# Chunk attention followed by a two-layer MLP: the same 1459 steps in another written order, and wider filler matmuls

## The chip, the cores and the metric

The kernel runs on one core of one Trainium2 chip. A core has a matrix engine (PE, with its weight loads shown as PEld), a vector engine (DVE), a scalar engine (ACT), a general engine (POOL), and a sync engine (SP) that issues transfers. POOL issues transfers too: each of its load instructions keeps POOL busy while it runs. The metric is the device time of one execution in microseconds (us); the time before is the median of three runs.

## The reference: what is computed

`q`, `k` and `v` have 8 batches, 8 heads, 576 rows and 64 columns. Attention is done inside chunks of 64 rows only, and its output, written as 4608 tokens of 512 columns, goes through two dense layers with a leaky ReLU between them:

```
scores = (q_c @ k_c.T) / sqrt(64)            # per chunk of 64 rows
attn   = exp(scores - max); attn /= sum + 1e-9
x      = (attn @ v_c) as 4608 tokens x 512
h      = x @ w_in                            # 512 -> 2048
out    = max(0.01 * h, h) @ w_out            # 2048 -> 512
```

## The kernel before: tiles, stages and what sets the order

**Attention.** The 4608 tokens are 36 groups of 128 tokens, numbered u = 0 to 35. A group passes through a fixed chain of steps, and the texts below use these names:

- the loads of q and k by POOL (L96), which cast from 4 to 2 bytes on the way; v comes per batch into `VB` (L120), for the first four groups per group into `v_t` (L126);
- the transposes of q and k: for u below 10 on PE (L410 for q, L415 for k; PSUM tiles `qp` and `kp`), after that as DMA transposes that SP issues (L438 for q into `QT`, L441 for k into `KT`); a copy puts q into the padded tile `QZ` (on POOL, L454, for u of 10 and above);
- s(u), the scores on PE (tile `Sp`, L466 and L473); then on DVE and ACT the row maximum, the subtraction, the exponential, the row sum, its reciprocal, and n(u), the scaling (tile `en`, L527, on DVE or POOL);
- the transpose of `en` into `et`: on PE (L535) for u below 8 and for u = 8, 9, 18, 27, 29, 31, and as a DMA transpose by SP (L546) for the others; this one is called d(u);
- v(u), the product with v on PE (tile `xp`, L558 and L571), whose result ACT or DVE copies into `xT`.

**The MLP.** The tokens are also cut into twelve blocks: four of 128 tokens, then eight of 512. The weights come as four column blocks of `w_in`, each in two halves (L135, 256 KB a half), and four blocks of `w_out` (L141, 512 KB each). Blocks 0 to 3 do plain products (L187 for the first layer, L215 for the second). Blocks 4 and 5 do the first layer plainly; from there on each layer of a block is done with seven products of halves in place of eight (L328 and L377), with sums of halves formed on DVE or POOL (L237, L240).

**The order.** Nothing is scheduled at run time. The program builds a list of 1459 steps, each with an engine; a table `ON` names the engine for those steps that could run on several. A second table, `ORDER`, is a written list: one entry per step with the step's number, the amount of filler to issue ahead of it, and the PSUM banks that it takes. `run` (L633) walks through it and emits the steps. An engine executes its own instructions in that order, so an entry says what stands ahead of what in the queue of its engine, and nothing else: SP's list is the order of the DMA transposes and of the stores, POOL's list is the order of the loads and of POOL's own work.

**Fillers.** `idle` (L590) issues matmuls of a constant tile of ones into a PSUM bank that nobody reads. They stand only in the first 20 us, ahead of PE steps that wait for their input.

```
(66, (13, 0), 0)    # step 66: the transpose of q of group 0, behind 13 filler matmuls into bank 0
```

Of the kernel before, what the change touches and what calls it, by code (L numbers as in the profile page):

```python
# [16 lines left out]
def kernel(  # L17
# [9 lines left out]
    nc = tc.nc  # L27
# [123 lines left out]
    ones = XF[0][:, 0, 0, :128]  # L151
# [15 lines left out]
    def bank(shape, name, tag):  # L167
        return psp.tile(shape, FP32, name=name, tag=tag, bufs=1)
# [421 lines left out]
    def idle(n, tag):  # L590
        t = bank([128, 4, 128], "idle", tag)
        for i in range(n):
            nc.tensor.matmul(out=t[:, i % 4, :], lhsT=ones, rhs=ones, start=True, stop=True)
# [95 lines left out]
    def arrive_v(b, c0, c1, after=(), **kw):  # L689
# [9 lines left out]
        ('ze', 0): 'dve', ('n', 0): 'dve', ('d2', 0): 'act', ('a', 0): 'act', ('out', 0, 0): 'act', ('p', 1, 0): 'act', ('k', 1): 'dve', ('ze', 1): 'act',  # L699
        ('n', 1): 'dve', ('d2', 1): 'act', ('a', 1): 'act', ('p', 2, 0): 'act', ('p', 2, 1): 'act', ('k', 2): 'act', ('ze', 2): 'act', ('n', 2): 'dve', ('d2', 2): 'dve',  # L700
        ('a', 2): 'act', ('out', 2, 0): 'act', ('p', 3, 0): 'dve', ('p', 3, 1): 'dve', ('k', 3): 'act', ('ze', 3): 'act', ('n', 3): 'dve', ('d2', 3): 'dve',
        ('a', 3): 'act', ('out', 3, 0): 'act', ('p', 4, 0): 'dve', ('p', 4, 1): 'act', ('k', 4): 'act', ('ze', 4): 'act', ('n', 4): 'dve', ('d2', 4): 'dve',
# [535 lines left out]
    for j in range(len(BLOCKS)):  # L1238
        groups((START[j] + BLOCKS[j]) // G)
        w = BLOCKS[j] / 512  # L1240
# [26 lines left out]
        for h, n in enumerate(parts):  # L1267
            p0, w = place + h / per_h, 1 / per_h
# [47 lines left out]
```

## Time and profile before

| what | value |
|---|---|
| median of 3 runs | 283.37 us (283.05 to 284.16) |
| the profiled execution, whole | 282.36 us |
| its span, first to last instruction | 280.6 us |
| PE busy in the span | 266.1 us (95%), 3480 matmuls |
| of it fillers | 96 matmuls, 8.6 us |
| DVE, ACT, POOL busy | 217.8, 177.8, 171.9 us |
| loads issued by POOL | 18.09 MB written, queue q0 |
| transposes and stores issued by SP | queue q1, 46544 packets |

The span is 1.8 us shorter than the execution's own time, because the time also holds what lies around the first and last instruction. In a line of the timeline the first number is the start from the span's beginning and the second how long the instruction or the run of equal instructions took; a bracket gives the idle time of the engine ahead of it and what ended it. In a table of stretches each engine has its busy time and, in brackets, its number of instructions.

### The profile page before, as it was taken

What the parts mean: (1) busy time and instruction counts of PE and PEld (TensorE: products, weight loads), DVE (VectorE), ACT (ScalarE), POOL (GpSimd) and SP (SyncE); (2) the same over time, 40 slices, a digit from 0 to 9 for tenths busy, and PEclk for the clock granted to TensorE, in tenths of its full rate; (3) what the DMA queues carried; (4) which work ended last, traced back from release to release, by engine and by line L of the source; (5) the groups of instructions that cost most, each with busy time, mean ns of one, the idle gap of its engine ahead of it and who ended that gap; (6) DMA issues with size and microseconds to landing.
All of it is one profiled execution on the core that took longest, in us unless ns stands there. A gap on an engine that the chain in (4) does not pass through costs nothing.

```text
span 280.6 us, 8400 instructions
## 1 busy us (share of the span) xinstructions
PE 266.1 (95%) x3480; PEld 239.3 (85%) x3480; DVE 217.8 (78%) x368; ACT 177.8 (63%) x356; POOL 171.9 (61%) x209
## 2 busy tenths in 40 slices
PE   4969999999999899998799999999999999999994
PEld 4859677889999799997799999998899999887883
DVE  3764357785898778999679998999899987688951
ACT  4464574878743476796588745999887765353412
POOL 8989965978999256695888387880763220350000
PEclk9997999999999999999999999999999999999999
DMA  9999999999999999999999999999992410002064
GB/s 129 140 164 195 179 172 172 130 157 171 169 139 157 136 131 134 197 184 120 156 140 176 151 175 140 169 295 146 113 138 21 168 22 18 2 0 77 0 227 151
DMA packets 162021, 38.29 MB, mean 136 GB/s; under 512 B 153024, under 2 KB 157632, under 8 KB 161984
## 3 DMA queue, kind: packets, MB, share of 16 engines
q0 software_dynamic: 114400, 18.09, 97.1%
q1 hardware_dynamic: 46544, 19.41, 44.2%
q8 instruction: 27, 0.44, 0.7%
q10 hardware_dynamic: 1040, 0.26, 0.4%
q14 instruction: 10, 0.08, 0.1%
HBM read 36.70 MB, written 9.44 MB: 164 GB/s over the span
## 4 chain that ended last, share of the span: by engine, by line
PE 73%; POOL 10%; DMA 10%; DVE 3%; issue 1%; ACT 1%; POOLq 0%; DVEq 0%
PE oA L377 15%; PE hA L328 14%; PE hT L187 10%; PE oC L377 9%; PE hC L328 7%; PE oP L215 5%; PE hB L328 4%; DMA KT<-k_in 4%; DMA w_inT<-in_moe_w_in_dram 3%; PE oB L377 3%; DMA et<-en 3%; POOL q_in L96 3%; POOL k_in L96 3%; PE Sp L473 2%; PE xp L571 2%; POOL QZ L454 2%
## 5 line engine op out<-in xcount | busy, mean ns | idle before, releaser
L377 PEld LDWEIGHTS <-gT 128*128 128x128 f16 x640 | 61.2, 98 | 6.7
L187 PE MATMUL hT<-xT,w_inT 128*128 128x128 f16 x768 | 48.5, 221 | 2.0 <-DMA w_inT<-in_moe_w_in_dram 2.0
L454 POOL COPY QZ<-QT 64x512 f16<-64x512 f16 x52 | 35.0, 674 | 21.2 <-DMA QT<-q_in 19.3
L187 PEld LDWEIGHTS <-w_inT 128*128 128x128 f16 x768 | 44.8, 99 | 2.8 <-issue 2.3
L328 PEld LDWEIGHTS <-VF 128*128 128x128 f16 x512 | 39.9, 98 | 3.7 <-issue 0.8
L527 POOL TENSOR_TENSOR en<-ex,zi 128x512 f16<-128x512 f16 x20 | 21.4, 1071 | 27.7 <-DVE zi L519 11.5
L240 DVE TENSOR_TENSOR tmp<-hC,tmp 128x512 f32<-128x512 f32 x48 | 32.1, 680 | 7.1 <-PE hC L328 4.3
L483 DVE TENSOR_REDUCE mx<-Sp 128x8 f32<-128x512 f32 x36 | 24.8, 688 | 15.8 <-PE Sp L473 14.4
L199 ACT ACTIVATE gT<-hT 128x512 f16<-128x512 f32 x48 | 27.0, 597 | 13.3 <-PE hT L187 12.7
L96 POOL DMA_DIRECT2D k_in<-in_k_dram x39 | 33.4, 862 | 2.1 <-ACT gT L199 1.2
L96 POOL DMA_DIRECT2D q_in<-in_q_dram x39 | 33.5, 863 | 1.2 <-DMA q_in<-in_q_dram 0.8
L377 PE MATMUL oA<-WF,gT 128*128 128x256 f16 x256 | 32.4, 273 | 0.0
L328 PEld LDWEIGHTS <-w_inT 128*128 128x128 f16 x384 | 29.9, 98 | 2.6 <-issue 0.5
L130 ACT ACTIVATE tmp<-hA 128x512 f32<-128x512 f32 x43 | 24.8, 597 | 10.5 <-PE hA L328 10.4
L493 ACT ACTIVATE ex<-sh 128x512 f16<-128x512 f32 x36 | 22.8, 632 | 8.5 <-DVE sh L487 8.3
L505 DVE TENSOR_REDUCE z<-ex 128x8 f32<-128x512 f16 x36 | 24.4, 678 | 4.2 <-ACT ex L493 4.1
L328 PE MATMUL hA<-XF,VF 128*128 128x128 f16 (+1 forms) x256 | 26.8, 246 | 0.6 <-DVE hB L132 0.6
L377 PEld LDWEIGHTS <-S 128*128 128x128 f16 x256 | 24.4, 98 | 2.6
L130 ACT ACTIVATE xT<-xp 128x512 f16<-128x512 f32 (+1 forms) x34 | 17.9, 548 | 13.6 <-PE xp L558 6.8
L487 DVE TENSOR_TENSOR sh<-Sp,mx 128x512 f32<-128x512 f32 x36 | 24.7, 685 | 0.5
L130 ACT ACTIVATE tmp<-oA 128x512 f32<-128x512 f32 (+1 forms) x16 | 8.6, 542 | 19.1 <-PE oA L377 19.1
L120 POOL DMA_DIRECT2D VB<-in_v_dram x16 | 17.7, 1105 | 4.3 <-PE xp L571 2.9
(93 smaller groups left out, 524.8 us busy)
## 6 DMA issues: line engine op xcount, KB each, us to landing
out_dram<-osb SPq DMA_DIRECT2D x14, 512.0 KB, 6.0
VB<-in_v_dram POOLq DMA_DIRECT2D x14, 288.0 KB, 12.2
q_in<-in_q_dram POOLq DMA_DIRECT2D x31, 128.0 KB, 10.4
k_in<-in_k_dram POOLq DMA_DIRECT2D x31, 128.0 KB, 9.6
w_inT<-in_moe_w_in_dram POOLq DMA_DIRECT2D x8, 256.0 KB, 8.7
w_outT<-in_moe_w_out_dram POOLq DMA_DIRECT2D x4, 512.0 KB, 8.5
out_dram<-osb SPq DMA_DIRECT2D x6, 256.0 KB, 4.8
v_t<-in_v_dram POOLq DMA_DIRECT2D x4, 128.0 KB, 6.5
```

The source lines that it names most:

```text
L96: nc.gpsimd.dma_start(out=t[a - u * G:z - u * G], in_=src[b, :, r:r + z - a, :].rearrange("h p d -> p h d"))
L130: nc.scalar.activation(out=to, in_=of, func=AFT.Copy, bias=0.0, scale=1.0)
L187: nc.tensor.matmul(out=hT[:, i, :], lhsT=w_inT[:, t, fc * 128:(fc + 1) * 128], rhs=xT[:, t, r0 % RING:r0 % RING + tb], start=(i == 0 and t ...
L199: nc.scalar.activation(out=to, in_=of, func=AFT.Prelu, bias=0.0, scale=1.0, alpha=0.01)
L240: (nc.vector if e == "dve" else nc.gpsimd).tensor_tensor(out=to, in0=a, in1=b, op=ALU.add)
L328: nc.tensor.matmul(out=PA[key][:, c, :], lhsT=w[:, t, fc * 128:(fc + 1) * 128], rhs=x[:, t, :], start=(m in (1, 5) and c == 0 and t == 0), ...
L377: nc.tensor.matmul(out=to, lhsT=lhs[:, fc, p * 128:(p + 1) * 128], rhs=rhs[:, fc, :], start=(fresh and fc == 0), stop=(fc == HB - 1), skip ...
L454: nc.gpsimd.tensor_copy(out=QZ[u % NQZ][part, :, :, s, :], in_=QT[u][part].rearrange("p i (e t) -> p i e t", e=2))
L483: nc.vector.tensor_reduce(out=MX[u], in_=SP[u], axis=AXL.X, op=ALU.max)
L487: nc.vector.tensor_tensor(out=SH[u], in0=SP.pop(u), in1=MX.pop(u).unsqueeze(2).to_broadcast((128, 8, CH)), op=ALU.subtract)
L493: nc.scalar.activation(out=E[u], in_=SH.pop(u), func=AFT.Exp, bias=0.0, scale=SCL)
L505: nc.vector.tensor_reduce(out=Z[c[0]][:, u - c[0]], in_=E[u], axis=AXL.X, op=ALU.add)
```

## The change

The steps, their arithmetic and their sizes stay. Three things differ.

**The filler.** The tile of ones grows from 128 to 512 columns (one memset in place of one), and an amount n is issued as single matmuls of up to four units of 128 columns:

```diff
-    ones = XF[0][:, 0, 0, :128]
+    ones = XF[0][:, 0].rearrange("p t n -> p (t n)")
     nc.vector.memset(ones, 1.0)
...
     def idle(n, tag):
-        t = bank([128, 4, 128], "idle", tag)
-        for i in range(n):
-            nc.tensor.matmul(out=t[:, i % 4, :], lhsT=ones, rhs=ones, start=True, stop=True)
+        t = bank([128, 512], "idle", tag)
+        while n:
+            w = min(n, 4) * 128
+            nc.tensor.matmul(out=t[:, :w], lhsT=ones[:, :128], rhs=ones[:, :w], start=True, stop=True)
+            n -= w // 128
```

The amounts: before 13, 1, 6, 8, 4, 5, 25, 15 and 19 (96 units, 96 matmuls); after 17, 8, 20, 9, 23, 14, 22 and 13 (126 units, 35 matmuls).

**The engines.** 95 of the entries of `ON` differ: 36 steps go from DVE to ACT and 36 from ACT to DVE, 12 from POOL to DVE and 9 from DVE to POOL, one from ACT to POOL and one back. Those that the prediction names:

```diff
-        ('n', 5): 'pool'
+        ('n', 5): 'dve'
...
-        ('n', 14): 'dve'
+        ('n', 14): 'pool'
...
-        ('sf', 9, 3): 'dve'
+        ('sf', 9, 3): 'pool'
...
-        ('sf', 10, 3): 'pool'
+        ('sf', 10, 3): 'dve'
```

(`sf` is the sum of halves of a whole block's activations, 128 x 2048, that opens or closes a second-layer product.)

**The order.** `ORDER` is replaced as a whole; its first lines as an example:

```diff
     ORDER = [
-        (51, 0), (10, 0), (6, 0), (2, 0), (1, 0), (35, 0), (0, 0), (37, 0), (36, 0), (66, (13, 0), 0), (7, 0), (50, 0), (40, 0), (68, (1, 1), 1), (67, 0), (43, 0),
-        (3, 0), (69, 0), (45, 0), (70, (6, 2), 2), (11, 0), (71, 0), (12, 0), (98, (8, 3), 3), (72, 0), (5, 0), (99, 0), (9, 0), (73, 0), (96, (4, 4), 4), (126, 0, 5),
...
+        (1, 0), (3, 0), (50, 0), (6, 0), (10, 0), (35, 0), (2, 0), (37, 0), (36, 0), (0, 0), (43, 0), (66, (17, 0), 0), (68, 0, 1), (45, 0), (7, 0), (67, 0), (40, 0),
+        (69, 0), (15, 0), (70, (8, 2), 2), (8, 0), (98, 0, 3), (71, 0), (46, 0), (126, 0, 4), (12, 0), (72, 0), (51, 0), (11, 0), (73, 0), (99, 0), (48, 0),
...
```

Read with the step numbers resolved, the lists of the engines differ in these places. POOL's first entries (q3 is the load of q of group 3, w0b the second half of `w_in` block 0, P0 block 0 of `w_out`, v8 a chunk of batch 0's v; memsets left out):

| | order of POOL's first loads |
|---|---|
| before | v_t1, q2, identity, k1, q1, k2, v_t0, q3, k3, w0b, w1b, w0a, w1a, q4, v_t2, w2b, v8b, w2a, P0, k4, P1, v_t3, q5, k5 |
| after | k1, v_t0, q2, v_t1, identity, q1, k2, v_t2, w1a, k3, q3, w0b, w0a, w2a, w1b, q4, q5, k5, w2b, P0, v8b, k4, P1, v_t3 |

PE's list from the first MLP product (A/B is block A, column block B of the first layer):

| | order on PE |
|---|---|
| before | 0/0, v(1), 0/1, q4 transposed, `en` of group 2 transposed, 1/0, v(2), 1/1, s(3), 2/0, 2/1, then 0/2 |
| after | v(1), 0/0, k3 transposed, `en` of group 2 transposed, 1/0, v(2), q4 transposed, 0/1, s(3), 2/1, 2/0, 1/1, then 0/2 |

SP's list between 84 and 129 us of the profile before (tk17 is the DMA transpose of k of group 17, tq that of q, store4b the second store of block 4):

| | order on SP |
|---|---|
| before | tk15, tk16, d11, tq17, d12, d13, d14, tk17, tq18, tk18, tq19, d15, tq20, tk19, store4a, tk20, tq21, store4b, d16, tk21, tq22, d17, tk22, d19 |
| after | tk15, d11, tk16, d12, tq17, d13, tk17, tq18, d14, tk18, d15, tq19, tq20, tk19, store4a, tk20, tk21, tq21, d16, tq22, d17, tk22, store4b, d19 |

Ahead of that, tk11 goes from in front of the stores of blocks 2 and 3 to behind them. On PE between 60 and 140 us the products with v and the scores move by up to 2.9 us of PE work against the MLP products around them: v(10) 1.98 us earlier, v(11) 1.79 us later, v(14) 2.89 us later, v(15) 2.89 us earlier, s(21) 1.97 us earlier, s(22) 0.87 us earlier (sums of the PE work that passes from one side of the step to the other, in the durations of the profile before).

More of the change, by code (lines that the diff above doesn't have):

```diff
@@ L694 @@
     ON = {
[4 rows of a table removed]
[L699 to L702, printed above, removed]
[55 rows of a table removed]
[4 rows of a table added]
+        ('d2', 0): 'act', ('a', 0): 'act', ('out', 0, 0): 'act', ('p', 1, 0): 'act', ('k', 1): 'dve', ('ze', 1): 'act', ('n', 1): 'dve', ('d2', 1): 'act',
+        ('a', 1): 'act', ('p', 2, 0): 'act', ('p', 2, 1): 'dve', ('k', 2): 'act', ('ze', 2): 'act', ('n', 2): 'dve', ('d2', 2): 'dve', ('a', 2): 'act',
+        ('out', 2, 0): 'act', ('p', 3, 0): 'dve', ('p', 3, 1): 'act', ('k', 3): 'act', ('ze', 3): 'dve', ('n', 3): 'dve', ('d2', 3): 'dve', ('a', 3): 'dve',
+        ('out', 3, 0): 'act', ('p', 4, 0): 'act', ('p', 4, 1): 'act', ('k', 4): 'dve', ('ze', 4): 'dve', ('n', 4): 'dve', ('d2', 4): 'act', ('a', 4): 'act',
[56 rows of a table added]
     }
     ORDER = [
[102 rows of a table removed]
[102 rows of a table added]
     ]
```

319 rows, old and new, of tables (ON, ORDER) are left out of this document.

## The prediction

> **What bounds the kernel now.** I read the page first, then the busy time by stretch, then the places on PE's timeline where a bracket shows idle time, and last what those waits lead back to on SP and POOL.
>
> ```profile
> PE 266.1 (95%) x3480; PEld 239.3 (85%) x3480; DVE 217.8 (78%) x368; ACT 177.8 (63%) x356; POOL 171.9 (61%) x209
> ...
> DMA  9999999999999999999999999999992410002064
> ```
>
> PE is the bound, and the transfer engines are busy in every slice up to about 210 us. Written order can't change PE's useful work, so the question is where PE is not busy:
>
> ```profile
> core 0: us, PE busy (x) PEld busy (x) DVE busy (x) ACT busy (x) POOL busy (x), PEclk, DMA share, GB/s
> 0.00:18.00 18.00, 13.28 (x192) 11.37 (x192) 10.86 (x25) 9.37 (x18) 16.81 (x27) 1.00 1.41 139
> 18.00:25.00 7.00, 5.44 (x91) 5.13 (x92) 2.23 (x6) 1.44 (x6) 5.78 (x9) 0.76 1.59 189
> 25.00:92.00 67.00, 67.00 (x1002) 58.12 (x1001) 48.41 (x81) 44.28 (x91) 57.74 (x71) 1.00 1.93 162
> 92.00:100.00 8.00, 6.72 (x108) 6.06 (x105) 5.89 (x12) 3.69 (x8) 2.79 (x5) 1.00 1.69 141
> 100.00:125.00 25.00, 25.00 (x406) 24.14 (x404) 22.23 (x41) 18.76 (x38) 17.04 (x22) 1.00 1.77 162
> 125.00:140.00 15.00, 12.66 (x193) 11.51 (x191) 11.83 (x20) 9.78 (x21) 10.78 (x12) 1.00 1.71 139
> 140.00:250.00 110.00, 110.00 (x1272) 100.27 (x1270) 95.91 (x159) 80.44 (x161) 59.78 (x69) 1.00 1.29 120
> 250.00:255.00 5.00, 4.06 (x36) 3.34 (x35) 4.96 (x7) 2.84 (x6) 1.18 (x1) 1.00 0.28 102
> ```
>
> There are four places. The start: loads have not come, and the clock was 0.76 between 18 and 25 us. Then 8.00 - 6.72 = 1.28 us between 92 and 100, 15.00 - 12.66 = 2.34 us between 125 and 140, and 5.00 - 4.06 = 0.94 us between 250 and 255. Everywhere else up to 255 us PE is full and nothing can be gained, only lost. So the change is worth at most 1.28 + 2.34 + 0.94 = 4.56 us behind the start, plus what the start gives.
>
> The change has three parts that can reach these places: the front (loads and fillers), the transfers and PE steps between 60 and 140 us, and the block sums near the end.
>
> **The front.** The fillers go from 96 units in 96 matmuls to 126 units in 35.
>
> ```profile
> 11.71 1.57 PE L593 MATMUL idle<-XF 128*128 128x128 f16 x25
> ...
> 19.15 1.05 PE L187 MATMUL hT<-xT,w_inT 128*128 128x128 f16 x16 [1.63 <-DMA w_inT<-in_moe_w_in_dram]
> ...
> 22.53 0.63 PE L410 MATMUL qp<-ident,q_in 128*128 128x128 f16 x4
> ...
> 25.98 3.74 PE L187 MATMUL hT<-xT,w_inT 128*128 128x128 f16 x64
> 29.56 1.03 PE L215 MATMUL oP<-w_outT,gT 128*128 128x512 f16 x4
> ```
>
> A filler unit costs 1.57 / 25 = 0.063 us, so 30 more cost 1.9 us of PE. They stand ahead of steps that wait anyway: the first MLP block began at 19.15 only because `w_in` had not landed, behind 1.63 us of idle PE. That wait covers them; without it the 1.9 us would be on the path. I take 0, with 0 to 0.4 should one batch outlast its wait.
>
> What decides is the order of POOL's loads. At the entry "0/2" of PE's list both versions have done the same useful steps, so its start compares the two fronts. Before, 64 matmuls take 29.56 - 25.98 = 3.58 us, a block of 16 takes 0.895, and 0/2, the third of them, starts at 25.98 + 2 x 0.895 = 27.77. After, PE reaches the transposition of q4 behind 0/0 and 1/0, and q4's load now has two more loads ahead of it, a `v_t` (128 KB) and a half block of `w_in` (256 KB):
>
> ```profile
> w_inT<-in_moe_w_in_dram POOLq DMA_DIRECT2D x8, 256.0 KB, 8.7
> ...
> v_t<-in_v_dram POOLq DMA_DIRECT2D x4, 128.0 KB, 6.5
> ```
>
> ```profile
> 10.92 9.81 DMA w_inT<-in_moe_w_in_dram
> ```
>
> The load just ahead of q4 landed at 10.92 + 9.81 = 20.73, and q4's 128 KB take 0.7 to 0.9 us more at the 189 and 139 GB/s of the stretches, so it was there at about 21.5. Another 384 KB at those rates are 2.1 to 2.8 us: 23.6 to 24.3 after. From there PE has q4's transposition, s(3) and four blocks: 2 x 0.23 + 4 x 0.895 = 4.04 us. 0/2 then starts at 27.6 to 28.3. I take 28.2, so the front loses 0.4 us. The bounds: with no wait for q4, the blocks start when `w_in` block 0 is there, 19.15 plus 0.7 for the `v_t` now ahead, and 6 x 0.895 + 5 x 0.23 = 6.5 us later it is 26.4 (a gain of 1.4); with q4 only at 22.53, when PE asked for it, plus 2.8, it is 29.4 (a loss of 1.6).
>
> **Transfers and PE steps from 60 to 140 us.** The waits, each on a DMA transpose:
>
> ```profile
> 91.65 0.40 PE L571 MATMUL xp<-et,VB 128*128 128x64 f16 x8
> ...
> 93.39 0.39 PE L473 MATMUL Sp<-KT,QZ 128*128 128x64 f16 x8 [0.47 <-DMA KT<-k_in]
> 93.62 1.91 PE L377 MATMUL oB<-w_outT,gT 128*128 128x256 f16 x16
> 96.35 0.39 PE L571 MATMUL xp<-et,VB 128*128 128x64 f16 x8 [0.81 <-DMA et<-en]
> ...
> 135.44 0.39 PE L473 MATMUL Sp<-KT,QZ 128*128 128x64 f16 x8 [1.50 <-DMA KT<-k_in]
> ```
>
> They are v(10) (no wait), s(15), v(11) and, for most of the second place, s(22). (s takes 93.62 - 93.39 = 0.23 start to start.) After, d11 is one place earlier on SP and v(11) is asked for 1.79 us of PE work later, so its 0.81 goes. s(15) is asked for 0.87 us earlier with its transpose in the same place, which would make its 0.47 up to 1.3. v(10) is 1.98 us earlier: d10 was issued at 82.06 and, at the median of 8.7 below, landed at 90.8, but v(10) is now wanted at 89.7. Unless SP runs ahead, about 1.1 us stays. So this place gives between 0 and 1.28; I take 0.8.
>
> For s(22) the path is SP's list:
>
> ```profile
> 82.06 2.51 SPq L546 DMA_TRANSPOSE et<-en  x1
> ...
> 94.10 4.26 SPq L546 DMA_TRANSPOSE et<-en  x2
> 98.41 1.26 SPq L441 DMA_TRANSPOSE KT<-k_in  x1
> ...
> 101.12 3.04 SPq L441 DMA_TRANSPOSE KT<-k_in  x1
> ...
> 115.50 0.60 SPq L389 DMA_DIRECT2D out_dram<-osb  x1
> 116.21 3.73 SPq L546 DMA_TRANSPOSE et<-en  x1
> ...
> 125.29 2.26 SPq L441 DMA_TRANSPOSE KT<-k_in  x1
> ```
>
> ```profile
> 125.29 10.11 DMA KT<-k_in
> ```
>
> ```profile
> DMA to landing us min/median/max: 7.4/8.7/11.3
> ```
>
> The last line is that of the `et` transposes from 80 to 136 us. A DMA transpose is issued in about 1.26 when nothing holds it (the row at 98.41). The two of d13 and d14 fill 4.26 us, so SP stood about 4.26 - 2 x 1.26 = 1.7 us waiting for group 14's `en`, with tk17 and tq18 queued behind it; from 98.41 it goes almost without pause to tk22 at 125.29, which landed 10.11 later, at 135.40, 0.04 before s(22). After, tk17 and tq18 stand ahead of d14 and fill that hole: up to 1.7 us. The store store4b (0.7 from start to next start) moves behind tk22, and its 512 KB, which at 162 GB/s are 3.2 us of the transfer engines, leave the time ahead of tk22. Against this, issues of 3.04 and 3.73 show that SP is also held by transfers not yet through. Bounds: 0 to 1.7 + 0.7 + 3.2 = 5.6 us earlier. The nearest rows are the hole and the store's own slot, so I take 1.7 + 0.7 = 2.4, and 133.0 for the landing. s(22) is wanted 0.87 us of PE work earlier, so up to there PE stands 2.4 - 0.9 = 1.5 us better than before. Waits that end on one landing don't add: this 1.5 already holds the front's 0.4 and the 0.8 above. With nothing earlier on SP it is 0.9 worse; with all waits gone it is 1.28 + 2.34 - 0.4 = 3.2 better. Past 140 us the transposes had room in the profile, and PE coming 1.5 us sooner should leave most of it.
>
> The Trainium skill, "DMA: Bandwidth & Descriptors", section "Queues, rings and completion order", says that each transfer engine takes turns between the queue rows it has work for, so a store on SP's own row is served ahead of the transposes behind it. By that rule the whole 3.2 us would count and the sum would be the far bound; the long issues agree with a crowded row, but no row here separates the store's share.
>
> **The end.** The 0.94 us lead back to a block sum on POOL:
>
> ```profile
> 247.12 4.06 POOL L237 TENSOR_TENSOR gT<-gT,S 128x2048 f16<-128x2048 f16 x1 [3.96 <-DVE S L237]
> ...
> 249.31 2.42 DVE L201 SCALAR_TENSOR_TENSOR gT<-tmp 128x512 f16<-128x512 f32 x1
> 252.25 0.68 DVE L201 SCALAR_TENSOR_TENSOR gT<-tmp 128x512 f16<-128x512 f32 x1
> 254.92 0.60 PE L328 MATMUL hA<-XF,VF 128*128 128x256 f16 x4 [0.63 <-DVE hB L132]
> ```
>
> The same DVE instruction took 2.42 beside the POOL sum and 0.68 after it: 1.74 us lost on DVE, and PE waited for DVE's later copies. After, this sum is DVE's own, and it stands behind the copy that PE waited for. I take a gain of 0.7 (0 to 0.94).
>
> **Sum.** 1.5 + 0.7 = 2.2 us, on the profiled execution 282.36 - 2.2 = 280.2. That execution is 1.0 below the median of 283.37, so the forecast for the median is 281.2 us.
>
> **Rivals.**
> *A. The waits all go.* If the store's traffic counts and the front doesn't wait, the gain is 1.4 + 1.28 + 2.34 + 0.94 = 6.0 at the very most; with the front at -0.4 it is 4.2, and 279.2. For it: PE is full everywhere else. Against: v(10) and s(15) are asked for earlier than d10 and tk15 landed.
> *B. The chain of transposes doesn't move.* If the transfer engines, busy in every slice, set the landings, tk22 lands at 135.4 as before; PE is 0.9 worse there and 0.7 better at the end: 283.6, no change.
> *C. Slower: the transposes take longer.* n(5) leaves POOL, so the loads behind it issue sooner and share the engines with the transposes. If tk22 has the longest time of the `et` row from the old issue time, 11.3 and not 10.11, it lands 1.2 later; PE at s(22) is 0.9 + 1.2 = 2.1 worse, less 0.7: 284.8. It decides once the landing slips by over 1.2 us.
> *D. The hold moves along.* The sum of block 9 now goes to POOL, and there the 1.74 us that DVE lost can stop PE instead: 281.2 + 1.7 = 282.9. The Trainium skill, "SBUF — State Buffer", section "SBUF: two separate sides", has this rule: DVE and POOL share a port pair as an exclusive lock for a whole instruction. The rows above agree (DVE's 2.42 ended 0.55 after the POOL sum). Against it, the sum is needed late.
>
> **Chances and range.** The forecast 44%, its own range 279.8 to 282.4; A 15%, B 18%, C 15%, D 8%. What a measurement can tell from no change is 0.5%, 1.4 us: faster is below 281.95, slower above 284.8. Faster: 0.38 of the forecast's 0.44, A, and 0.03 of B and D: 0.56. Slower: 0.12 of C and 0.04 of a bad front: 0.16. The same: 0.28. The range for 8 in 10 goes from 278.6, into A, to 285.0, just over C.
>
> **What would show it.** Right: 0/2 starts on PE between 27.6 and 28.6; tk17 is issued directly behind d13, tk22 at about 123 and s(22) starts near 133; the idle PE time from 125 to 140 falls from 2.34 to about 1, that from 250 to 255 to under 0.3; no stretch that was full shows a hole over 0.5 us. Wrong: PE waiting in the front beyond 29, tk22 issued no earlier than 125, a new wait at v(15) (wanted 2.89 us earlier) or behind the POOL sum of block 9.

## The result, and the profile after

The changed kernel takes 280.9 us (median of 20 executions) and the kernel before, beside it on the same chip, 282.7 (20 executions). The ratio is 0.9938, 95% interval 0.9909 to 0.9966: a gain of 1.75 us, between 1.0 and 2.6. The profiled execution took 279.45 us, 2.91 less than the 282.36 of before. That ratio leaves out executions more than 1.5% above the fastest of their kernel; the kernel before spreads by more than that by itself, in part for a reason that the experiments show (in their first series 18 of its 35 executions would go, and the changed kernel would come out at 0.999), so for them the mean of all executions is given, as a difference from the kernel before on the same chip in the same series, with a 95% interval.

The stretches of the changed kernel, in the columns of the prediction's table:

```profile
25.00:92.00 67.00, 66.26 (x990) 56.91 (x987) 50.00 (x88) 41.14 (x80) 54.80 (x64) 1.00 1.92 165
92.00:100.00 8.00, 8.00 (x125) 7.60 (x122) 5.56 (x13) 3.44 (x7) 2.91 (x4) 1.00 1.43 144
100.00:125.00 25.00, 25.00 (x405) 24.10 (x403) 22.01 (x39) 20.40 (x43) 22.37 (x29) 1.00 1.82 147
125.00:140.00 15.00, 15.00 (x242) 14.36 (x239) 14.08 (x24) 12.54 (x25) 12.59 (x14) 1.00 2.04 184
140.00:250.00 110.00, 109.25 (x1238) 99.14 (x1237) 92.71 (x153) 80.65 (x159) 60.30 (x66) 1.00 1.18 125
250.00:255.00 5.00, 5.00 (x48) 4.50 (x46) 4.33 (x6) 2.80 (x6) 0.00 (x0) 1.00 0.00 0
```

Before, PE stood still for 4.56 us between 25 and 255 us. Now the 3.62 us between 92 and 140 and the 0.94 at 250 are gone, and 67.00 - 66.26 = 0.74 us between 25 and 92 and 0.75 us between 140 and 250 are new: 1.49. The difference, 3.07 us, is nearly the whole 3.0 us by which the span fell. So in these two executions the front gave nothing. The row of the chain of waits that sets it, and its rows on PE's timeline:

```profile
15.93 7.66 DMA q_in<-in_q_dram
...
23.72 0.38 PE L410 MATMUL qp<-ident,q_in 128*128 128x128 f16 x4 [0.37 <-DMA q_in<-in_q_dram]
...
25.07 4.63 PE L187 MATMUL hT<-xT,w_inT 128*128 128x128 f16 x80
```

q4 landed at 15.93 + 7.66 = 23.59 and PE waited 0.37 us for it. 0/2 is the fourth of the five blocks from 25.07: 25.07 + 3 x 0.895 = 27.75, against 27.77 before.

SP's timeline; then the last line of the view of `KT` between 121 and 122 us (the landing time of that one transpose), the same line for `et` from 80 to 136 us, and s(22) on PE:

```profile
95.84 1.19 SPq L546 DMA_TRANSPOSE et<-en  x1
97.14 2.00 SPq L441 DMA_TRANSPOSE KT<-k_in  x1
99.24 1.21 SPq L438 DMA_TRANSPOSE QT<-q_in  x1
100.55 1.22 SPq L546 DMA_TRANSPOSE et<-en  x1
...
121.34 1.78 SPq L441 DMA_TRANSPOSE KT<-k_in  x1
123.18 0.58 SPq L389 DMA_DIRECT2D out_dram<-osb  x1
```

```profile
DMA to landing us min/median/max: 8.4/8.4/8.4
...
DMA to landing us min/median/max: 3.8/7.5/9.3
...
131.38 0.40 PE L473 MATMUL Sp<-KT,QZ 128*128 128x64 f16 x8
```

tk17 (97.14) stands directly behind d13 (95.84), and d14 behind tq18. tk22 is issued at 121.34 (125.29 before), lands 8.4 us later at 129.75 (135.40 before), and s(22) runs at 131.38 with no bracket: nothing was waited for.

The three largest waits that the changed kernel has of its own behind the front, and the DVE and POOL rows at the third:

```profile
59.19 1.95 PE L187 MATMUL hT<-xT,w_inT 128*128 128x128 f16 x32 [0.16 <-DVE KT L132]
...
65.84 1.05 PE L187 MATMUL hT<-xT,w_inT 128*128 128x128 f16 x16 [0.52 <-ACT xT L130]
...
230.54 0.60 PE L328 MATMUL hC<-xT,VF 128*128 128x256 f16 x4 [0.75 <-DVE tmp L240]
```

```profile
225.27 4.07 POOL L237 TENSOR_TENSOR gT<-gT,S 128x2048 f16<-128x2048 f16 x1
...
228.09 1.80 DVE L201 SCALAR_TENSOR_TENSOR gT<-tmp 128x512 f16<-128x512 f32 x1
```

The first two are copies on DVE and ACT that now stand behind other work. The third is the block sum of block 9, now on POOL: beside it a DVE instruction took 1.80 us.

### The profile page after: what moved, and what is told of

It reads as the page before. It is cut to its first block, busy times and chain, and to the rows that moved or that the text cites. A ratio compares the mean times of both kernels' runs of the same rounds, so it can differ in the third digit from the quotient of the medians.

```text
span 277.6 us, 8288 instructions
## 1 busy us (share of the span) xinstructions
PE 265.4 (96%) x3419; PEld 234.4 (84%) x3419; DVE 218.2 (79%) x372; ACT 180.8 (65%) x355; POOL 174.2 (63%) x206
## 4 chain that ended last, share of the span: by engine, by line
PE 87%; POOL 5%; DMA 3%; DVE 2%; issue 1%; ACT 1%; DVEq 0%; POOLq 0%; ACTq 0%
PE oA L377 20%; PE hA L328 15%; PE hT L187 15%; PE oC L377 10%; PE hC L328 8%; PE oB L377 5%; PE oP L215 5%; PE hB L328 4%; PE Sp L473 3%; DMA q_in<-in_q_dram 3%; PE xp L571 2%; POOL q_in L96 1%; POOL w_inT L135 1%; POOL k_in L96 1%; PE tpe L535 1%
## 5 line engine op out<-in xcount | busy, mean ns | idle before, releaser
L454 POOL COPY QZ<-QT 64x512 f16<-64x512 f16 x52 | 39.3, 762 | 14.6 <-DMA QT<-q_in 12.7
L187 PE MATMUL hT<-xT,w_inT 128*128 128x128 f16 x768 | 47.5, 219 | 0.7 <-ACT xT L130 0.5
L130 ACT ACTIVATE tmp<-hA 128x512 f32<-128x512 f32 x44 | 25.5, 599 | 7.6 <-PE hA L328 6.5
L505 DVE TENSOR_REDUCE z<-ex 128x8 f32<-128x512 f16 x36 | 24.3, 675 | 3.1 <-ACT ex L493 2.9
L130 ACT ACTIVATE xT<-xp 128x512 f16<-128x512 f32 (+1 forms) x35 | 19.1, 561 | 9.6 <-PE xp L571 9.0
L199 ACT ACTIVATE gT<-tmp 128x512 f16<-128x512 f32 x36 | 22.1, 630 | 2.1 <-DVE tmp L240 2.1
## 6 DMA issues: line engine op xcount, KB each, us to landing
VB<-in_v_dram POOLq DMA_DIRECT2D x14, 288.0 KB, 10.3
```

The costliest lines, as they stand in the source:

```text
L130: nc.scalar.activation(out=to, in_=of, func=AFT.Copy, bias=0.0, scale=1.0)
L187: nc.tensor.matmul(out=hT[:, i, :], lhsT=w_inT[:, t, fc * 128:(fc + 1) * 128], rhs=xT[:, t, r0 % RING:r0 % RING + tb], start=(i == 0 and t ...
L199: nc.scalar.activation(out=to, in_=of, func=AFT.Prelu, bias=0.0, scale=1.0, alpha=0.01)
L454: nc.gpsimd.tensor_copy(out=QZ[u % NQZ][part, :, :, s, :], in_=QT[u][part].rearrange("p i (e t) -> p i e t", e=2))
L505: nc.vector.tensor_reduce(out=Z[c[0]][:, u - c[0]], in_=E[u], axis=AXL.X, op=ALU.add)
```

## The experiments

In the table, 0/2 is its start in the profile, the next three numbers are PE's idle time in the profile from 25 to 92, from 92 to 140 and from 140 to 255 us, and the last is the mean of all executions against the kernel before, with the number of executions in brackets (the kernel before had a mean of 282.63 beside the first 20, and of 282.36, 282.17, 283.55 and 282.68 in the four series, of 35, 33, 11 and 11 executions).

| kernel | 0/2 | PE idle, us | mean against before, us |
|---|---|---|---|
| before | 27.77 | 0 / 3.62 / 0.94 | |
| changed | 27.75 | 0.74 / 0 / 0.75 | -1.9 ± 0.8 (20) |
| changed, again | 27.56 | 0.74 / 0.94 / 0.86 | -1.3 ± 0.7 (12) |
| changed, block sum of 9 on DVE | 27.34 | 0.74 / 0.97 / 0.46 | -2.2 ± 0.9 (12) |
| before, SP's list new | 26.01 | 0 / 0.89 / 2.56 | -2.5 ± 0.8 (12) |
| changed, SP's list old | 27.72 | 0.74 / 2.10 / 1.99 | +1.7 ± 1.7 (12) |
| before, more filler | 28.01 | 0.56 / 2.86 / 0.94 | -1.5 ± 0.8 (12) |
| before, SP's list new but for the store | 25.98 | 0.36 / 1.62 / 2.75 | -1.4 ± 0.8 (10) |
| changed, no filler | 27.75 | 1.48 / 0.25 / 1.55 | -1.0 ± 1.1 (10) |
| changed, q4 earlier | 27.78 | 0.74 / 0.94 / 1.22 | one execution |
| combined | 28.09 | 1.54 / 0.96 / 0.94 | -3.0 ± 1.0 (10) |
| combined, wide fillers | 25.58 | 0.06 / 2.78 / 0 | -3.8 ± 1.1 (4) |
| combined, tuned | 25.83 | 0.76 / 0.46 / 1.99 | -4.3 ± 1.2 (6) |
| best | 25.8 | 0.14 / 0.61 / 0.60 | -4.5 ± 1.4 (6) |

**The changed kernel again.** No edit.

> The changed kernel a second time. If its profile is typical, PE stands still in the same places: ahead of q4's transposition near 23.7 us (0.4 us), near 59 and 66 us (0.2 and 0.5 us) and near 230 us (0.75 us), nowhere between 92 and 140 us, and the span is 277 to 279 us. If the vanished waits between 92 and 140 us were this one execution's luck, some 0.5 to 2 us of them come back and the span is 279 to 280 us.

```profile
125.63 0.41 PE L473 MATMUL Sp<-KT,QZ 128*128 128x64 f16 x8 [0.94 <-POOL QZ L454]
```

q4, 59, 66 and 230 us are as in the first profile, but between 92 and 140 us PE waited 0.94 us, for POOL's copy of q of group 20. The same wait stands in four of the five profiles with the changed PE list and fillers; the first one is the exception. So the first profile was a lucky one. The five waits of the kernel before are gone in both, and with the new one some 2.7 of the 3.62 us are gained.

**The block sum of block 9 on DVE.**

```diff
-        ('sf', 9, 3): 'pool'
+        ('sf', 9, 3): 'dve'
```

> The changed kernel with the block sum of block 9 on DVE instead of POOL. Theory (the hold moved along with the sum): the DVE instruction that took 1.80 us beside the POOL sum takes 0.7, PE's wait of 0.75 us near 230 us is gone, and the span is 0.7 to 0.9 us shorter than the changed kernel's. Rival (DVE has no room there): DVE's copies come 1.2 us later, PE waits for them by 0.5 us or more at the same place, and nothing is gained.

```profile
226.74 1.22 DVE L237 TENSOR_TENSOR gT<-gT,S 128x2048 f16<-128x2048 f16 x1
...
229.07 0.68 DVE L201 SCALAR_TENSOR_TENSOR gT<-tmp 128x512 f16<-128x512 f32 x1
...
228.61 0.41 PE L571 MATMUL xp<-et,VB 128*128 128x64 f16 x8 [0.34 <-DVE tmp L240]
```

The sum takes 1.22 us on DVE, the later instruction 0.68 instead of 1.80, and PE's 0.75 at 230 us becomes 0.34 at a nearby step. Both sides were half right: the hold had moved along with the sum, and DVE had room for most but not all of it. The kernel is 0.9 ± 0.8 us below the changed one in the same series.

**SP's list alone, put into the kernel before**, and **the old list put into the changed kernel.** From 84 to 129 us (the rest of the list goes over too, with some 17 moved entries elsewhere):

```diff
-tk15, tk16, d11, tq17, d12, d13, d14, tk17, tq18, tk18, ... store4b, d16, tk21, tq22, d17, tk22, d19
+tk15, d11, tk16, d12, tq17, d13, tk17, tq18, d14, tk18, ... tk21, tq21, d16, tq22, d17, tk22, store4b, d19
```

> The kernel before with only SP's list (transposes and stores) as in the changed kernel; fillers, loads, engines and PE's order as before. Theory (SP's list carries the gain between 92 and 140 us): the transpose of k of group 22 is issued near 122 and lands near 131 to 132, PE's idle time between 92 and 140 us falls from 3.6 to 0.5 to 1.5 us, and the time is 2 to 3 us below before. Rival (PE's order, and POOL without n of group 5, carry it): the idle time stays at 3 us or more and the time is within 0.7 us of before.

> The changed kernel with SP's list as in the kernel before; everything else as changed. Theory (SP's list carries the gain): the transpose of k of group 22 is issued at 124.5 or later, PE stands still 1.5 to 3 us between 92 and 140 us, and the time is 1.5 to 3 us above the changed kernel. Rival (the rest carries it): under 0.7 us of idle time there and the time of the changed kernel within 0.7 us.

The first rows are of the kernel before with the new list, the rows in the second fence of the changed kernel with the old one:

```profile
24.23 3.74 PE L187 MATMUL hT<-xT,w_inT 128*128 128x128 f16 x64
...
120.53 1.26 SPq L441 DMA_TRANSPOSE KT<-k_in  x1
...
DMA to landing us min/median/max: 9.3/9.3/9.3
```

```profile
99.87 1.27 SPq L441 DMA_TRANSPOSE KT<-k_in  x1
...
124.57 1.21 SPq L441 DMA_TRANSPOSE KT<-k_in  x1
...
133.98 0.39 PE L473 MATMUL Sp<-KT,QZ 128*128 128x64 f16 x8 [0.66 <-ACT xT L130]
```

tk22 goes out at 120.5 and 121.3 with the new list, at 124.6 and 125.3 with the old; over all profiles here it is 120.3 to 123.3 with the new list and 124.6 to 125.6 with the old. In the first pair 1.8 of the 4.8 us are the front's (0/2 at 26.01 against 27.77). In the second pair 0/2 is the same; there tk17 already goes out 2.73 us sooner (97.14 against 99.87), so most of the 3.2 us is the hole. With the new list in the kernel before, the idle time from 92 to 140 us falls from 3.62 to 0.89, while that behind 140 us rises from 0.94 to 2.56; with the old one in the changed kernel the first rises to 2.10. (The last bracket names a copy, but tk22 took 9.3 us there too and landed at 133.9: s(22) waited for that.) SP's list carries this gain. With it alone the kernel before is even faster than the whole change (-2.5 against -1.3 in one series), so the rest of the change costs 1.2 ± 0.7 us, net.

**The store's share.** The new list in the kernel before, with one entry left where it was:

```diff
-... tk21, tq21, d16, tq22, d17, tk22, store4b, d19
+... tk21, tq21, store4b, d16, tq22, d17, tk22, d19
```

> The kernel before with SP's list as in the changed kernel, except that the second store of block 4 stays ahead of the transpose of en of group 16. It tells the store's share. If only its slot on SP counts, the transpose of k of group 22 is issued 0.5 to 0.8 us later than with the whole list (120.5), lands near 130.5, and the time is within 0.7 us of 279.5. If its 512 KB of traffic count too, the transpose lands 2 to 4 us later than with the whole list (129.8), s(22) waits 1 us or more again, and the time is 280.5 to 281.5.

```profile
113.12 1.34 SPq L438 DMA_TRANSPOSE QT<-q_in  x1
114.55 0.55 SPq L389 DMA_DIRECT2D out_dram<-osb  x1
115.19 3.64 SPq L546 DMA_TRANSPOSE et<-en  x1
...
122.19 1.63 SPq L441 DMA_TRANSPOSE KT<-k_in  x1
...
DMA to landing us min/median/max: 8.8/8.8/8.8
```

tk22 goes out 1.66 us later than with the whole list, of which 1.09 were there before the store was reached (tq21 at 113.12 against 112.03), and takes 8.8 us to land, not longer than the 9.3 without the store. So for tk22 the store cost its slot, 115.19 - 114.55 = 0.64 us. Its 512 KB may show on d16, directly behind it, which landed 11.0 us after its issue against 10.3 without the store; v(16) waited 0.48 us for it, and s(22) for nothing. The time, 280.85 us in the median, is in the range that was expected if the traffic counts, but the late landing of tk22 and the wait at s(22) that were to make it so did not come. The two kernels ran in different series and differ by 1.1 ± 1.1 us against the kernel before, so the times don't decide.

**More filler in the kernel before.**

```diff
-(82, 0, 7)          # step 82: 0/0
+(82, (20, 7), 7)
```

> The kernel before with 20 more filler units (1.3 us of PE) in the wait ahead of the first MLP product at 19.15 us, nothing else. Theory (the fillers matter through the clock): of 35 executions of the kernel before 16 have a mean granted clock of about 0.994 and take 1.9 us longer on the mean than the 19 others; 0.006 of 280 us is one stretch of 3.4 us at half clock, such as that from 20.47 to 23.88 us in its profile. With PE busy in that wait no execution is at 0.994, PE's entry 0/2 starts near 26.0 us and not 27.8, and the median is 0.8 to 1.5 us below that of before. Rival (the clock falls whatever PE does there): as many executions at 0.994 as before, and the median within 0.5 us of before.

The stretch of half clock in the kernel before, and the same stretch here:

```profile
20.47:23.88 3.41, 3.01 (x29) 3.04 (x30) 0.26 (x1) 0.92 (x3) 2.83 (x5) 0.50 1.44 197
```

```profile
20.47:23.88 3.41, 3.06 (x64) 2.73 (x62) 0.56 (x2) 1.15 (x3) 2.63 (x5) 1.00 1.49 180
```

PE gets through 64 matmuls where it got through 29. Of the 90 executions of the kernel before in the four series, 39 have a mean clock of 0.994 or less (mean time 283.4 us), 51 of 0.997 or more (281.7); here none of 12 is low, and in the changed kernel 1 of 32. The median moved by 1.0 us (280.88 against 281.89). The clock part of the theory holds. 0/2 did not come sooner in this profile: the first product, which waits for the load of `w_in`, began at 19.97 against 19.15 (in the profiles with this front and narrow fillers it varies from 18.89 to 19.97), and PE stood 0.56 us with no releaser shown, as in the combined kernel below.

**No filler in the changed kernel.**

```diff
-(66, (17, 0), 0) ... (110, (13, 6), 6, 7)
+(66, 0, 0) ... (110, 0, 6, 7)          # all eight
```

> The changed kernel without any filler matmul (126 units left out; they compute nothing that is read). Theory (the fillers keep the clock up): most executions show a mean clock of 0.995 or less, 0/2 starts 1 us or more later than 27.6 in such a profile, and the time is 1 to 3 us above the changed kernel's 281. Rival (two batches outlast their wait, by about 0.6 us, and the rest does nothing): clock as before, 0/2 at 27.0 to 27.6, time within 0.7 us of the changed kernel's.

```profile
DMA to landing us min/median/max: 6.6/6.8/6.9
...
19.48 1.89 PE L187 MATMUL hT<-xT,w_inT 128*128 128x128 f16 x16
...
23.71 0.40 PE L410 MATMUL qp<-ident,q_in 128*128 128x128 f16 x4
...
25.07 4.63 PE L187 MATMUL hT<-xT,w_inT 128*128 128x128 f16 x80
```

The first line is that of q4's two halves, issued at 15.2 and 15.9 us. Up to 23 us PE runs at half speed (the block at 19.48 takes 1.89 us; one takes 1.07 at full clock), although the granted clock in the profile's rows is 1.00 there and no execution has a low mean clock. And yet 0/2 starts at 27.75, as with the fillers, and the time is the same within what can be told. The way there is another, though: q4 landed at 15.9 + 6.6 = 22.5 us, and PE came to its transposition only at 23.71, behind its own slow steps; with the fillers PE was there first and waited for q4. So the rival was right that the mean clock and the time stay, and the theory was right that PE runs slower without the fillers. In this front the two ends meet, to the hundredth by chance, and the fillers buy nothing that the time shows.

**The changed front with q4 earlier.** q4's load moves from behind `w0a, w2a, w1b` to behind `w0a`, and two amounts are cut:

```diff
-..., w0a, w2a, w1b, q4, ...     (108, (22, 4), 4) (110, (13, 6), 6, 7)
+..., w0a, q4, w2a, w1b, ...     (108, (12, 4), 4) (110, (10, 6), 6, 7)
```

> The changed kernel with q4's load two half blocks of w_in earlier (behind the first half of block 0), and 13 filler units fewer in the two batches that outlast their wait (22 to 12, 13 to 10). Theory (q4's landing behind the moved loads sets the changed front): PE's q4 transposition doesn't wait, and 0/2 starts at 26.6 to 27.1 us instead of 27.3 to 27.8. Rival (the load of w_in block 1, now later, takes its place): 0/1 waits for it and 0/2 stays at 27.3 or later.

```profile
22.51 0.40 PE L410 MATMUL qp<-ident,q_in 128*128 128x128 f16 x4
23.96 1.07 PE L187 MATMUL hT<-xT,w_inT 128*128 128x128 f16 x16 [1.06 <-DMA w_inT<-in_moe_w_in_dram]
...
25.10 4.63 PE L187 MATMUL hT<-xT,w_inT 128*128 128x128 f16 x80
```

q4 no longer waits (22.51), and 0/1 waits 1.06 us for the half block that is now behind it: 0/2 at 25.10 + 3 x 0.895 = 27.78. The rival was right; the one execution took 281.26 us.

**Combined.** The kernel before with SP's new list, the 20 units of filler, and two sums on DVE (the block sum of block 10 and an input sum of block 8):

```diff
-        ('sf', 10, 3): 'pool', ('xf', 8, 0, 2): 'pool'
+        ('sf', 10, 3): 'dve', ('xf', 8, 0, 2): 'dve'
```

> The kernel before with three things: SP's list as in the changed kernel, 20 more filler units ahead of the first MLP product, and two sums of halves on DVE instead of POOL (the block sum of block 10, and one of the input sums of block 8, on which PE waited 1.1 us near 169 with SP's new list). PE's order, the loads and their order stay those of before. By the parts: 279.5 for the SP list, less 0.4 for the clock, 1.3 for the block sum and 1.1 for the input sum: 276.7. Rival (the waits move to the next transpose or copy): 278.5 to 279.5.

```profile
27.65 2.39 PE L187 MATMUL hT<-xT,w_inT 128*128 128x128 f16 x40 [1.54 <-issue]
```

It missed the sum by 2.8 us (279.5 in the median against 276.7). The wait at 250 us is gone; the one that the kernel before with SP's new list has near 169 us only changed its releaser, DVE for POOL; and PE stood 1.54 us in the middle of a block, eight matmuls in, where it waits for no tile.

**Wide fillers in the combined kernel.** `ones` and `idle` as in the change; the amounts stay.

> The combined kernel (before with SP's new list, 20 more filler units, two sums on DVE), its fillers now as single matmuls of up to 512 columns, the same units: 34 filler matmuls for 116. In the combined kernel PE stood still 1.5 us in the middle of an MLP product near 27 us, with no releaser shown, while the PE's own instructions (packets of 16 KB, 256 instructions each) came late: the packet that PE asked for arrived at 26.2 us, with 697 PE instructions begun. Theory (PE ran out of loaded instructions): 164 instructions fewer ahead of that point take the stall away, 0/2 starts near 26.4 us and not 28.1, and the time is 1 to 1.7 us below 279.5. Rival (the stall has another cause): it stays, 0/2 near 28, time within 0.5 us of 279.5.

```profile
23.80 3.74 PE L187 MATMUL hT<-xT,w_inT 128*128 128x128 f16 x64
...
106.60 0.52 PE L571 MATMUL xp<-et,VB 128*128 128x64 f16 x8 [2.78 <-DMA et<-en]
```

```profile
106.50:110.00 3.50, 3.40 (x29) 2.91 (x30) 0.00 (x0) 1.20 (x3) 2.03 (x2) 0.53 1.71 154
```

The stall is gone, the four blocks run in one piece and 0/2 starts at 23.80 + 2 x 0.895 = 25.6, 2.5 us sooner, 1.5 of it the stall. The span did not follow (278.0 against 278.1 us), and the times can't tell the two kernels apart: v(14) now waits 2.78 us for d14, and the 3.4 us after that run at half clock. In this profile, what was won in front was lost at the next transpose.

**Tuned, and best.** SP's and POOL's lists (i8 is an input sum of block 8, one of which was on DVE in the combined kernel; L31 a load of group 31), then two more entries of SP's:

```diff
-SP: d13, tk17, tq18, d14             POOL: ..., L31, load of v, i8
+SP: d13, tk17, d14, tq18             POOL: ..., i8, i8, L31, load of v
-SP: tq28, tq29, d25, tk28, tk29, d26
+SP: tq28, tq29, tk28, tk29, d25, d26
```

> As the combined kernel with wide fillers, and two waits that it still had: on SP the transpose of en of group 14 goes ahead of that of q of group 18 (v(14) waited 1.1 us for it near 107), and the input sums of block 8 stay on POOL but ahead of two loads (PE waited 1.1 us near 171 for DVE). Theory (each of the waits is the last one at its place): 1.5 to 2.2 us less than the combined kernel with wide fillers, 276 to 277. Rival (what is behind them becomes late): less than 0.7 us of gain, with new waits of PE behind 107 us in the trace.

> The tuned combined kernel with two more entries of SP's list moved: the transposes of k of groups 28 and 29 go ahead of the transpose of en of group 25, for which SP stood 2.9 us (165.0 to 167.8) with those two behind it. Theory (a hole in SP's list is free room, as between 84 and 129 us): the two fill the hole, PE's wait of 1.5 us ahead of s(29) near 179.5 is gone, and the time is 0.7 to 1.7 us below the tuned kernel's 279.2. Rival (the transpose of en is now late, or PE waits at the next place): v(25) or a later step waits 0.7 us or more, and the time stays within 0.5 us of 279.2.

SP in the tuned kernel, then in the best:

```profile
161.52 3.46 SPq L438 DMA_TRANSPOSE QT<-q_in  x2
167.83 1.19 SPq L546 DMA_TRANSPOSE et<-en  x1
...
179.53 0.39 PE L473 MATMUL Sp<-KT,QZ 128*128 128x64 f16 x8 [1.50 <-DMA KT<-k_in]
```

```profile
161.79 3.89 SPq L438 DMA_TRANSPOSE QT<-q_in  x2
165.78 2.51 SPq L441 DMA_TRANSPOSE KT<-k_in  x2
168.39 5.02 SPq L546 DMA_TRANSPOSE et<-en  x2
```

The tuned kernel gained 0.5 us on the one before it, within what the few executions tell: v(14)'s wait went and s(29)'s came, as its rival said. The best one fills the hole from 165.0 to 167.8 with the two transposes; s(29) waits no more. PE's idle time from 25 to 255 us falls from 3.21 to 1.35. Against the kernel before the mean is only 0.2 us lower than the tuned one's, so the times don't tell what the last step gave. The best kernel takes 278.0 us (median of 6), by the means 0.984 of the kernel before (0.979 to 0.989): its gain is more than twice that of the change.

## Why the prediction was right, and where it was not

The time was within 0.3 us of the forecast (281.2 against 280.9), and the two largest terms have the right sign and mechanism. The gain was 1.75 us where 2.2 were forecast; the time came closer than that because the kernel before, too, was faster beside it (282.7) than in its first three runs (283.4). The agreement of the sum owes something to errors that cancel.

- **The front, -0.4 taken.** The chain was as described: two more loads ahead of q4, q4 landed at 23.59 (23.6 to 24.3 was worked out), and 0/2 started at 27.75 (27.6 to 28.3). The term was 0.0. Two errors cancel in q4's landing: before, the second half of its load was issued at 12.85 and took 9.2 us, so it landed at 22.05 and not at 21.5, and the two loads ahead of it then cost 1.5 us and not 2.1 to 2.8. That the fillers cost nothing held too: behind them PE stood 0.37 us for q4.
- **The missing term of the front.** The prediction read the clock of 0.76 between 18 and 25 us and gave it no price. The profiled execution of before had a half-clock stretch itself (mean clock 0.993), like the 39 of 90. Without one, that front has 0/2 at 25.98 and 26.01 in two profiles (SP's list new), where the four profiles of the changed front with its fillers have 27.34 to 27.75. So against full-clock executions the changed front loses 1.3 to 1.8 us, and against the others it loses nothing. In the time, the changed kernel gains by nearly never falling to half clock: 0.43 x (283.4 - 281.7) = 0.7 us on the mean. The front alone doesn't decide that: with SP's old list in the changed kernel 4 of 12 executions were low.
- **SP's list, 1.5 us better at s(22) taken, 0.9 worse to 3.2 better.** s(22) came 135.44 - 131.38 = 4.06 us sooner, 0.87 of that by its place in PE's list: 3.2 better in the profile, the far bound; some 2 with the wait that the second profile has. The mis-sized steps: tk22's issue (2.4 us sooner taken; 3.95 measured, but 1.9 to 3.2 against the changed kernel with the old list, over four profiles) and its flight, taken as unchanged at 10.1 and measured as 7.7 to 9.3 in the first four profiles with the new list. The hole in front of d14 was filled as described. The far bound's mechanism, the store's 3.2 us of traffic, is not what the runs show: for tk22 the store was worth its slot. What the prediction worked out beside it from the rule in the Trainium skill, "DMA: Bandwidth & Descriptors", section "Queues, rings and completion order", that each transfer engine takes turns between the queue rows, namely that the store's whole traffic would count, is not borne out: tk22's flight was 8.8 us with the store ahead and 9.3 without. tk22 is issued 7.6 us behind the store, so this tells nothing on the rule itself.
- **v(11), s(15), v(10).** All three ran without a wait in the first two profiles (0.8 of 1.28 was taken). For v(10) it was close: in the kernel without fillers it waited 0.74 us for d10.
- **"No stretch that was full shows a hole over 0.5 us".** Wrong. 0.74 us between 25 and 92 us stand in every profile of the changed kernel with its fillers and not in that of before. They come from DVE's and ACT's own order: a copy behind a weight sum of 1.2 us, another behind an exponential. The prediction named transfers and PE steps and took the other 90 moved engines as free.
- **The end, 0.7 taken.** The wait at 250 us went. Rival D came true beside it, with 0.75 us and not 1.7, a wait that the prediction had named as a sign of being wrong: the net is 0.94 - 0.75 = 0.2 us. "The sum is needed late" was no argument; what counts is what DVE does beside it. DVE's instruction took 1.80 us beside POOL's sum and 0.68 without it. The lock between the two that the Trainium skill states ("SBUF — State Buffer", section "SBUF: two separate sides") agrees with that.
- **Rivals A to C.** The waits of A did all go in the profiled execution, but 1.49 us of others came, and in the second profile 0.94 more. B is excluded by tk22's issue and landing, C by flights that became shorter: 7.5 us in the median for `et` against 8.7.

## What to carry to other kernels

An in-order queue that stands for one late input has a hole as long as that stand; putting ready entries into it moves all that follow, and this can be read from the queue's own timeline before anything is built. The list of one queue was worth more than the whole rewrite that it came with, so when a generated order changes everywhere, try its lists one by one. And look at the granted clock of many executions: a wait of PE under 2 us can cost as much again behind it, in some executions and not in others.

## What the runs showed of the hardware that was not expected

**The clock answers to waits of 1.6 us.** In the kernel before PE stood 1.63 us ahead of 19.15 us and the clock was halved from 20.47 to 23.88; in the wide combined kernel it stood 2.78 us and was halved for the next 3.4 us. 39 of 90 executions of one and the same program have the mean clock that goes with such a stretch (3.4 us at half clock in 280 are 0.006). Not every such wait does it: the 1.50 us ahead of s(22) in the kernel before were followed by none. The Trainium skill, "TensorE: Matmul & The Clock Gate", section "What's actually happening", says that the gate looks at windows of 3.4 us that run freely, not from the kernel's start. That agrees with the length of both stretches and fits the chance from one execution to the next; its table asks for an idle window, while here PE had been busy for 1.71 of the 3.42 us from 17.05 to 20.47:

```profile
17.05:20.47 3.42, 1.71 (x37) 1.32 (x35) 1.46 (x3) 1.26 (x4) 2.78 (x4) 1.00 1.71 174
```

**PE's own program comes through the transfer engines.** The page of the profile lists a queue of instructions; this is its line in the kernel before (packets, MB, share):

```profile
q8 instruction: 27, 0.44, 0.7%
```

27 packets for 2 x 3480 PE instructions are one for 258; the kernel without fillers has 26 for 2 x 3384. That the queue is PE's is inferred from that. In the kernels whose front ran fast with 96 or more narrow fillers PE stood 0.4 to 1.5 us near 27 us with no releaser, in three of four profiles; with the wide fillers, 166 instructions fewer, this was gone in front of 0/2 in all three. That PE ran out of loaded instructions there fits these profiles, but no run delays such a packet by itself, so it isn't proven.
